# Two unread half-precision products ahead of the scores of four attention steps

## The chip, the cores and the metric

The kernel runs on one core of one Trainium2 chip. The metric is the device time of one execution in microseconds (us); the time of a kernel is the median of several executions. Five engines work side by side, each through its own queue in order: TensorE (PE in the profile, its weight loads PEld), VectorE (DVE), ScalarE (ACT), GpSimd (POOL) and SyncE (SP), whose queue issues the DMA transfers. They meet at semaphores.

## What is computed

Attention over 4 batches, 8 heads, 576 positions of 64 elements, with a position bias that a small network makes out of the distance of two positions; and behind it a feed-forward block of 512 to 2048 to 512 with a squared relu, over all 2304 rows:

```python
scores = scale * np.matmul(q, k.transpose(0, 1, 3, 2))
x = (psi_rel / psi_i)[..., None]          # logs of distance and position
bias = np.maximum(x @ w1 + b1, 0.0) @ w2  # one number for each pair and head
scores = scores + bias.transpose(2, 0, 1)[None, :, :, :]
attn = np.exp(scores - np.max(scores, axis=-1, keepdims=True))
attn = attn / (np.sum(attn, axis=-1, keepdims=True) + 1e-09)
out = np.matmul(attn, v)
...
h = np.maximum(x @ w_in, 0.0)             # x: out, heads side by side
return (h * h @ w_out).astype(np.float32)
```

## The kernel before

The batches are taken in two pairs `p`; the rows of a pair are cut into five blocks `c` (block 0 holds the last 64 rows of both batches, blocks 1 to 4 hold 128 rows of each). A step `t` of the main loop is one (p, c, head); there are 80. The blocks of the first pair go in the order 0, 3, 2, 4, 1, so steps 0 to 7 are block 0, and steps 8 to 15 are block 3 with heads 0 to 7.

A step has these parts. `qk` makes the scores on PE: queries and keys are split into a high and a low half-precision part, and three products of parts are added (high by high, high by low, low by high). In block 0 that is line 413. In the other blocks the 64 columns in the middle of both batches come from line 419 (three products of 128 columns), and the 512 other columns of each batch from line 425 (six products of 512 columns, two at a time on the two halves of the array's rows). All of it goes to one PSUM tile `sc` of 1536 columns, three banks of 512. In a block other than 0 the columns 0 to 575 and 960 to 1535 are used; columns 576 to 959, in the middle bank, are not. There is one `sc`, so the scores of a step wait until DVE has read those of the step before.

`softmax_a` takes the scores with the bias (`s`, line 441, DVE) and the exponent (line 447, ACT). `softmax_b` makes the transpose of the result: in the first two blocks (steps 0 to 15) with float32 transposes on PE (`tp`, lines 459 and 463) that ACT copies out to `at` (lines 460, 464); in the later ones with half-precision parts (`a`, POOL lines 473 and 474) and a transposing DMA. `pv` (line 506), three steps later, multiplies with the values; in steps 0 to 15 in float32.

Beside the steps run the bias (tiles `hg` on DVE and ACT, lines 307 and 309; products `bp` on PE, line 348; copies `be` on ACT, line 369; a DMA to memory and back), the feed-forward block as soon as a block's rows are there (`hp`, line 560, then `g` on ACT, DVE and POOL, then `o`, line 583), and the splitting of the weights, 32 pieces in all: three DVE operations (`ci` lines 223 and 224, `cv` line 226), a cast on ACT (`winH`, `woutH`, line 129) and two POOL operations (scaling `cv` in place, line 131, and the low part, line 242). POOL also splits the values `v` of the first pair, which were read in float32: it casts the high part (`v`, half precision, line 131), scales the float32 tile in place (`v` on `v`, line 131), subtracts (line 154) and clears a corner (line 160). `cv`, the bias copies `be` and two tiles of the feed-forward block take their buffers from one pool of five. The scaling of values in place may only run when the product `pv` that still reads the float32 tile is done: head 0's after step 8's `pv`, head 1's after step 9's, and so on.

The order of the instructions in each queue isn't written by hand. The kernel is built with a scheduler that puts every instruction on an assumed timeline, by the priority `tc.cur_priority` at which it was written and the numbers in `PLACE`, and from that timeline come the queues' orders and the turn in which buffers are taken. An added instruction therefore may move others. `now[0]` is the step that is being written.

Of the kernel before, what the change touches and what calls it, by code (L numbers as in the profile page):

```python
# [51 lines left out]
def tile_attention_moe(  # L52
# [11 lines left out]
    nc = tc.nc  # L64
# [53 lines left out]
    sc = ps_sc.tile([128, 1536], F32, name="sc")  # L118

    now = [0]  # L120
# [281 lines left out]
    def qk(p, c, h):  # L402
        kt = k_t[p, h]
        qt = q_t[p, c, h // 4]
        if h % 4 == 3:
            q_t.pop((p, c, h // 4))
        qs = slice(128 * (h % 4), 128 * (h % 4) + 128)
        terms = ((0, 0), (0, 1), (1, 0))
        if c == 0:
            for n, (qz, z) in enumerate(terms):  # L410
                o = 960 * (h % 2)
                for c0, m in ((0, 64), (64, 512)) if h % 2 else ((0, 512), (512, 64)):
                    nc.tensor.matmul(out=sc[:, o + c0:o + c0 + m], lhsT=qt[:, qz, qs], rhs=kt[:, z, c0:c0 + m],  # L413
                                     start=(n == 0), stop=(n == 2))
        else:

            mid = sc[:, 512:1408].rearrange("p (b j) -> p b j", b=2)[:, :, 0:64]
            for n, (qz, z) in enumerate(terms):
                nc.tensor.matmul(out=mid, lhsT=qt[:, qz, qs], rhs=kz[:, (p * 8 + h) % NKZ, z, :],  # L419
                                 start=(n == 0), stop=(n == 2))  # L420

            for n, (qz, z) in enumerate(terms):
                for b in range(2):
                    r = slice(64 * b, 64 * b + 64)
                    nc.tensor.matmul(out=sc[:, 1024 * b:1024 * b + 512], lhsT=qt[r, qz, qs],  # L425
                                     rhs=kt[r, z, 64 * b:64 * b + 512],
                                     start=(n == 0), stop=(n == 2), tile_position=(64 * b, 0))
# [349 lines left out]
    for t in range(NS + LAG):  # L777
# [5 lines left out]
        if t < NS:  # L783
            p, c, h = steps[t]
            with place("qk"):
                qk(p, c, h)
            with place("sa"):
                softmax_a(p, c, h)
            if t + 2 < NS:
                bias_ld(*steps[t + 2])  # L790
            if h % 4 == 2 and t + 2 < NS:
                q_split(*qlist[(t + 2) // 4])
                q_next()
            if len(moe) > BACKLOG:
                moe_unit()
            softmax_b(p, c, h)
            if last < 0 or steps[last][2] != H - 1:
                moe_unit()
# [77 lines left out]
```

## Time and profile before

| | us |
|---|---|
| median of 3 executions | 655.32 (654.44 to 657.93) |
| the profiled execution | 661.45 |
| its span, first to last instruction | 659.70 |
| PE busy in the span | 615.1 (93%) |
| DVE, ACT, POOL busy | 407.1, 388.1, 376.5 |
| mean granted TensorE clock | 0.965 |

The span is read in two parts. Up to about 110 us DVE is busy nearly without a gap and PE has idle time; from there on PE has hardly any. [...] A row of the timeline gives the start, the time until the end of the last of its instructions, the engine, the line and how many instructions were merged; a bracket is idle time of the engine ahead of it, and what ended it.

### The profile page before, as it was taken

How to read it: one execution, taken by the hardware profiler on the slowest of the kernel's cores; microseconds unless marked ns; L12 is line 12 of the kernel's file. 1: busy time of each engine (PE TensorE's matmuls, PEld its weight loads, DVE VectorE, ACT ScalarE, POOL GpSimd, SP SyncE). 2: the span in 40 equal slices, each digit the busy share in tenths (PEclk: the TensorE clock that was granted, in tenths of full speed). 3: DMA queues.
4: the chain of work that ended last, by engine and by line, in shares of the span. 5: the costliest groups of instructions: out<-in, count | busy, mean ns of one | idle time of the engine just before them, and what ended most of it. 6: DMA issues, size and time to landing. Idle time of an engine off the chain costs nothing.

```text
span 659.7 us, 15574 instructions
## 1 busy us (share of the span) xinstructions
PE 615.1 (93%) x6056; PEld 394.8 (60%) x6056; DVE 407.1 (62%) x813; ACT 388.1 (59%) x856; POOL 376.5 (57%) x394
## 2 busy tenths in 40 slices
PE   5565798999899999999899999999999999999997
PEld 2223356766455566666576676676676676767664
DVE  7997999888864765585856447346545642632321
ACT  5587978788776476656656655656465564342111
POOL 2757578899665456756775465555464663432221
PEclk9698967999999999999899999999999999999999
DMA  7999888477876787889978778679787777524000
GB/s 237 278 294 319 268 255 248 155 209 178 197 173 152 162 193 176 179 180 226 221 170 158 167 134 174 140 169 153 139 172 134 154 149 155 122 56 86 17 34 16
DMA packets 206568, 112.16 MB, mean 170 GB/s; under 512 B 167072, under 2 KB 183456, under 8 KB 206496
## 3 DMA queue, kind: packets, MB, share of 16 engines
q1 hardware_dynamic: 206496, 111.19, 72.0%
q8 instruction: 47, 0.77, 0.5%
q14 instruction: 25, 0.20, 0.1%
HBM read 55.44 MB, written 15.61 MB: 108 GB/s over the span
## 4 chain that ended last, share of the span: by engine, by line
PE 69%; DVE 5%; DMA 4%; issue 2%; ACT 1%; POOL 1%; DVEq 0%; POOLq 0%; ACTq 0%
PE o L583 26%; PE hp L560 26%; PE pv L506 8%; PE sc L425 5%; PE bp L348 2%; DMA at<-a 2%; DVE hg L309 1%; PE sc L419 1%; PE sc L413 1%; DMA xt<-xh 1%; DMA stg<-vd 1%; DVE s L441 1%; DVE cv L226 0%; DVE ci L224 0%; ACT a L129 0%
## 5 line engine op out<-in xcount | busy, mean ns | idle before, releaser
L560 PE MATMUL hp<-xt,winH 128*128 128x256 f16 (+1 forms) x1280 | 195.9, 263 | 0.0
L583 PE MATMUL o<-woutH,g 128*128 128x512 f16 x576 | 185.6, 382 | 4.0 <-ACT o L590 2.2
L560 PE MATMUL hp<-xt,winL 128*128 128x256 f16 (+1 forms) x640 | 162.8, 263 | 0.0
L583 PEld LDWEIGHTS <-g 128*128 128x128 f16 x864 | 82.8, 98 | 97.0 <-issue 11.5
L560 PEld LDWEIGHTS <-winH 128*128 128x128 f16 x1280 | 117.0, 99 | 30.0 <-issue 13.6
L441 DVE CUSTOM_DVE_ANT_0 s<-sc,bt 128x576 f32<-128x576 f32 x144 | 103.5, 751 | 44.1 <-PE sc L425 34.2
L474 POOL TENSOR_TENSOR a<-s,a 128x1024 f16<-128x1024 f32 (+1 forms) x64 | 130.3, 2036 | 0.0
L568 DVE TENSOR_TENSOR r<-hp,r 128x512 f32<-128x512 f32 (+1 forms) x80 | 50.6, 632 | 118.7 <-ACT r L566 118.6
L570 POOL TENSOR_TENSOR g<-r,g 128x512 f16<-128x512 f32 (+1 forms) x80 | 86.7, 1084 | 59.1 <-DVE g L133 48.4
L447 ACT ACTIVATE s<-s,nm 128x576 f32<-128x576 f32 x144 | 111.3, 773 | 6.4
L583 PE MATMUL o<-woutL,g 128*128 128x512 f16 x288 | 109.8, 381 | 0.0
L473 POOL TENSOR_TENSOR a<-s,a 128x128 f16<-128x128 f32 (+1 forms) x64 | 28.1, 440 | 140.4 <-ACT a L129 135.5
L445 ACT ACTIVATE nm<-mx,esc 128x1 f32<-128x1 f32 x144 | 40.9, 288 | 110.8 <-DVE mx L441 110.5
L506 PE MATMUL pv<-v,at 128*128 128x64 f16 (+5 forms) x2112 | 97.9, 207 | 0.5 <-ACT at L460 0.5
L129 ACT ACTIVATE a<-s 128x1152 f16<-128x1152 f32 (+1 forms) x64 | 70.5, 1102 | 44.6 <-DMA at<-a 43.6
L566 ACT ACTIVATE r<-hp 128x512 f32<-128x512 f32 (+1 forms) x80 | 43.1, 539 | 49.6 <-PE hp L560 49.6
L506 PEld LDWEIGHTS <-at 128*128 128x128 f16 (+1 forms) x1792 | 58.3, 100 | 20.2 <-issue 8.6
L560 PEld LDWEIGHTS <-winL 128*128 128x128 f16 x640 | 62.9, 98 | 5.8
L309 DVE TENSOR_SCALAR hg<-tab_t 128x464 f32<-128x464 f32 (+17 forms) x86 | 58.9, 729 | 11.5 <-PE bp L348 11.4
L425 PE MATMUL sc<-k,q 64*128 64x512 f16 x384 | 55.6, 387 | 0.0
L369 ACT ACTIVATE be<-bp,hcst,rows_s 128x288 f32<-128x288 f32 (+29 forms) x67 | 35.8, 571 | 16.5 <-PE bp L348 11.1
L348 PE MATMUL bp<-hg,w2s 128*32 128x288 f32 (+15 forms) x152 | 36.1, 546 | 6.1 <-ACT hg L303 2.4
(88 smaller groups left out, 688.7 us busy)
## 6 DMA issues: line engine op xcount, KB each, us to landing
bt<-biasd SPq DMA_DIRECT2D x64, 288.0 KB, 3.3
stg<-w_in SPq DMA_DIRECT2D x16, 512.0 KB, 5.1
stg<-w_out SPq DMA_DIRECT2D x16, 512.0 KB, 4.7
bt<-biasd SPq DMA_DIRECT2D x32, 144.0 KB, 3.4
qst<-qd SPq DMA_DIRECT2D x32, 128.0 KB, 3.5
out<-o SPq DMA_DIRECT2D x16, 256.0 KB, 2.4
v<-vd SPq DMA_DIRECT2D x8, 320.0 KB, 4.9
stg<-vd SPq DMA_DIRECT2D x8, 320.0 KB, 4.3
```

Source lines behind the costliest of these rows:

```text
L129: nc.scalar.activation(out=out, in_=in_, func=AF.Copy, scale=scale)
L309: nc.vector.tensor_scalar(ht, src, scl[:, n:n + 1], None, op0=ALU.min)
L348: nc.tensor.matmul(out=bp[32 * t:32 * t + 32, 0:d1 - d0], lhsT=w2s if gi < 4 or PATS[z][t] == "A" else w2n, rhs=ts_[t][:, d0:d1], start=Tr ...
L425: nc.tensor.matmul(out=sc[:, 1024 * b:1024 * b + 512], lhsT=qt[r, qz, qs], rhs=kt[r, z, 64 * b:64 * b + 512], start=(n == 0), stop=(n == 2 ...
L441: nc.vector.tensor_tensor_reduce(s[:, 576 * b:576 * b + 576], sc[:, 960 * sb:960 * sb + 576], bt, inv, -3.0e38, ALU.add, ALU.max, mx[:, b: ...
L447: nc.scalar.activation(out=sl, in_=sl, func=AF.Exp, bias=nm[:, b:b + 1], accum_out=su[:, h, b:b + 1])
L474: nc.gpsimd.tensor_tensor(av[:, :, 640:1152], ev[:, :, 0:512], av[:, :, 0:512], op=ALU.subtract)
L506: nc.tensor.matmul(out=dst, lhsT=lhsT, rhs=vt[r, 5 * b + blk, :] if f32 else vt[:, vz, 5 * b + blk, :], start=(n == 0), stop=(n == nt - 1) ...
L560: nc.tensor.matmul(out=hp[:, f * T:f * T + T].rearrange("p (b t) -> p b t", b=nb), lhsT=wt[:, k, c0:c0 + 128], rhs=xt[:, 0:nb, z * 4 + k, ...
L568: nc.vector.tensor_tensor(rr, hp[:, 0:2 * T], rr, op=ALU.mult)
L570: nc.gpsimd.tensor_tensor(g[:, 1, 0:2 * T], r[:, 0:2 * T], g[:, 0, 0:2 * T], op=ALU.subtract)
L583: nc.tensor.matmul(out=blk["o"][b], lhsT=g[:, z, c0:c0 + 128], rhs=wt[:, 2 * u + f, :], start=(u == 0 and f == 0 and z == 0 and wt is wout ...
```

## The change

At the head of `qk`, before a step's scores, two products are added in steps 9 to 12 (block 3, heads 1 to 4): the high part of the queries (128 by 128) with the first 384 columns of the high part of the step's keys, half precision, over all 128 rows of the array, to columns 576 to 959 of `sc`. Nothing reads them.

```diff
         terms = ((0, 0), (0, 1), (1, 0))
+        if 9 <= now[0] < 13:
+            for _ in range(2):
+                nc.tensor.matmul(out=sc[:, 576:960], lhsT=qt[:, 0, qs], rhs=kt[:, 0, 0:384], start=True, stop=True)
         if c == 0:
```

So 8 products and 8 weight loads are added, and no instruction is removed. With them the scheduler gives other orders: PE's differ from step 9 to about step 23, DVE's, ACT's, POOL's and SP's from about step 11 to step 22; the later part of each queue is the same. In the changed program lines from 411 on have a number higher by 3.

On PE, around the scores of step 10 (with what each instruction waits for). Before:

```order
236 L463 MATMUL tp<-ident,s 64x128 [waits Activation_49]
237 L419 LDWEIGHTS q
238 L419 MATMUL sc<-kz,q 128x2x64 [waits DVE_49]
239 L419 LDWEIGHTS q
240 L419 MATMUL sc<-kz,q 128x2x64
```

And now:

```order
240 L466 MATMUL tp<-ident,s 64x128 [waits Activation_49]
241 L411 LDWEIGHTS q
242 L411 MATMUL sc<-k,q 128x384 [waits DVE_49]
243 L411 LDWEIGHTS q
244 L411 MATMUL sc<-k,q 128x384
245 L422 LDWEIGHTS q
246 L422 MATMUL sc<-kz,q 128x2x64
```

The two products (line 411) stand straight ahead of the scores (line 419, now 422), and the wait for DVE that the first score product had is now at the first of them. It is so in steps 9 to 12, in step 11 with one transpose between the two.

On DVE, between the softmax of step 12 (the first pair of line 441, now 444) and that of step 13 (the second pair). The numbers behind the names tell the pieces apart. Before:

```order
158 L441 ISA s_1421,mx_1422<-sc_141,bt_1208 128x576
...
162 L226 SCALAR_TENSOR_TENSOR cv_1180<-stg_1094,ci_1181 128x512
163 L309 TENSOR_SCALAR hg_1273<-tab_t_129 128x352 x2
164 L223 TENSOR_SCALAR ci_1277<-stg_1104 128x512
165 L224 SCALAR_TENSOR_TENSOR ci_1277<-stg_1104,ci_1277 128x512
166 L226 SCALAR_TENSOR_TENSOR cv_1276<-stg_1104,ci_1277 128x512
167 L223 TENSOR_SCALAR ci_1287<-stg_1178 128x512
168 L441 ISA s_1536,mx_1537<-sc_141,bt_1314 128x576
```

And now:

```order
153 L444 ISA s_1429,mx_1430<-sc_141,bt_1212 128x576
...
158 L226 SCALAR_TENSOR_TENSOR cv_1172<-stg_1019,ci_1173 128x512
159 L309 TENSOR_SCALAR hg_1277<-tab_t_129 128x352 x2
160 L223 TENSOR_SCALAR ci_1183<-stg_1094 128x512
161 L224 SCALAR_TENSOR_TENSOR ci_1183<-stg_1094,ci_1183 128x512
162 L226 SCALAR_TENSOR_TENSOR cv_1182<-stg_1094,ci_1183 128x512
163 L444 ISA s_1544,mx_1545<-sc_141,bt_1320 128x576
```

The softmax of step 13 now stands behind the piece from `stg_1094`; before, the next piece (`stg_1104`) and the first operation of the one after it stood ahead of it too: four operations of the splitting have moved behind it.

On POOL, behind the low part of the piece `cv_1086`. `v_332` and `v_414` are the float32 values of heads 1 and 2, which `pv` of steps 9 and 10 reads. Before:

```order
78 L242 TENSOR_TENSOR woutL_127<-cv_1086,woutH_126 128x512
79 L131 TENSOR_SCALAR cv_1096<-cv_1096 128x512
80 L242 TENSOR_TENSOR winL_125<-cv_1096,winH_124 128x2x256
81 L131 TENSOR_SCALAR cv_1170<-cv_1170 128x512
82 L131 TENSOR_SCALAR v_332<-v_332 128x640
83 L242 TENSOR_TENSOR winL_125<-cv_1170,winH_124 128x2x256
84 L154 TENSOR_TENSOR v_2054<-v_332,v_2054 128x640
85 L131 TENSOR_SCALAR cv_1180<-cv_1180 128x512
...
89 L131 TENSOR_SCALAR v_414<-v_414 128x640
```

And now:

```order
78 L242 TENSOR_TENSOR woutL_127<-cv_1086,woutH_126 128x512
79 L131 TENSOR_SCALAR v_332<-v_332 128x640
80 L154 TENSOR_TENSOR v_2062<-v_332,v_2062 128x640
81 L131 TENSOR_SCALAR cv_1096<-cv_1096 128x512
82 L160 MEMSET v_2062 64x2x64
83 L131 TENSOR_SCALAR v_2148<-v_414 128x640
84 L242 TENSOR_TENSOR winL_125<-cv_1096,winH_124 128x2x256
85 L131 TENSOR_SCALAR v_414<-v_414 128x640
```

The scaling of `v_414`, which waits for the product of step 10, comes after six instructions instead of ten; the weights' parts that stood ahead of it (from `cv_1170` and `cv_1180` on) come behind it.

## Rows read from the trace of the kernel before

**Rows 1.** The page: granted clock of TensorE in 40 slices, in tenths.

```profile
PEclk9698967999999999999899999999999999999999
```

**Rows 2.** Stretches of 10 us: PE, PEld, DVE, ACT, POOL busy (x instructions); PEclk, DMA, GB/s.

```profile
80.00:90.00 10.00, 7.59 (x41) 4.66 (x40) 9.97 (x23) 8.99 (x24) 4.97 (x5) 0.76 0.89 259
...
100.00:110.00 10.00, 7.87 (x47) 5.88 (x45) 9.83 (x18) 8.27 (x22) 8.29 (x9) 0.78 0.82 251
110.00:120.00 10.00, 10.00 (x76) 7.33 (x77) 7.78 (x15) 7.97 (x20) 8.53 (x13) 0.71 0.60 184
...
130.00:140.00 10.00, 9.02 (x79) 6.03 (x79) 9.83 (x18) 7.41 (x19) 9.53 (x12) 1.00 0.87 250
...
160.00:170.00 10.00, 8.82 (x113) 4.81 (x110) 10.00 (x17) 6.82 (x16) 9.85 (x10) 1.00 1.03 221
```

**Rows 3.** The same for the single microseconds in which the granted clock changes.

```profile
85.00:86.00 1.00, 1.00 (x7) 1.00 (x7) 1.00 (x3) 0.98 (x3) 0.92 (x1) 0.55 0.96 362
95.00:96.00 1.00, 1.00 (x6) 0.54 (x6) 0.93 (x3) 0.90 (x2) 1.00 (x2) 0.83 0.90 329
105.00:106.00 1.00, 1.00 (x13) 0.72 (x5) 0.96 (x3) 1.00 (x4) 0.94 (x1) 0.79 1.03 340
115.00:116.00 1.00, 1.00 (x14) 1.00 (x11) 0.90 (x4) 0.98 (x3) 1.00 (x1) 0.59 0.49 193
```

**Rows 4.** Timeline of PE: scores of steps 10 to 13, values' products, a wait.

```profile
80.58 0.82 PE L425 MATMUL sc<-k,q 64*128 64x512 f16 x6
...
93.44 1.46 PE L425 MATMUL sc<-k,q 64*128 64x512 f16 x5
...
101.47 0.61 PE L425 MATMUL sc<-k,q 64*128 64x512 f16 x4
...
103.53 0.66 PE L459 MATMUL tp<-ident,s 128*128 128x128 f32 x4 [1.29 <-ACT be L369]
...
108.46 2.42 PE L506 MATMUL pv<-v,at 128*128 128x64 f32 x10
111.25 1.46 PE L425 MATMUL sc<-k,q 64*128 64x512 f16 x6
...
118.06 1.47 PE L506 MATMUL pv<-v,at 128*128 128x64 f32 x10
```

**Rows 5.** Waits of PE from 72 to 105 us: total, times, longest.

```profile
PE tp L459 <- ACT be L369: 2.2, 2, 1.3
```

**Rows 6.** Timeline of DVE.

```profile
112.39 0.69 DVE L223 TENSOR_SCALAR ci<-stg 128x512 uint32<-128x512 uint32 x1
113.80 0.76 DVE L441 CUSTOM_DVE_ANT_0 s<-sc,bt 128x576 f32<-128x576 f32 x1 [0.71 <-PE tp L459]
...
118.25 1.51 DVE L309 TENSOR_SCALAR hg<-tab_t 128x336 f32<-128x336 f32 x2 [1.23 <-PE bp L348]
...
148.90 0.76 DVE L441 CUSTOM_DVE_ANT_0 s<-sc,bt 128x576 f32<-128x576 f32 x1 [1.99 <-PE tp L463]
...
151.50 0.42 DVE L568 TENSOR_TENSOR r<-hp,r 128x256 f32<-128x256 f32 x1 [1.15 <-ACT r L566]
```

**Rows 7.** Timeline of POOL.

```profile
101.41 1.38 POOL L242 TENSOR_TENSOR woutL<-cv,woutH 128x512 f16<-128x512 f32 x1
104.08 0.62 POOL L131 TENSOR_SCALAR cv<-cv 128x512 f32<-128x512 f32 x1 [1.29 <-ACT winH L129]
...
106.72 0.72 POOL L131 TENSOR_SCALAR v<-v 128x640 f32<-128x640 f32 x1
107.41 1.16 POOL L242 TENSOR_TENSOR winL<-cv,winH 128x512 f16<-128x512 f32 x1
108.53 1.50 POOL L154 TENSOR_TENSOR v<-v 128x640 f16<-128x640 f32 x1
110.62 0.62 POOL L131 TENSOR_SCALAR cv<-cv 128x512 f32<-128x512 f32 x1 [0.59 <-ACT woutH L129]
```

**Rows 8.** Waits of PE from 105 to 180 us: total, times, longest.

```profile
PE o L583 <- POOL g L570: 1.8, 2, 1.2
```

## Prediction

> **What bounds the kernel now.** I read the page's line of the granted clock first, then the busy times in stretches of 10 us, then the timelines of PE, DVE and POOL in the stretch that the change touches.
>
> From about 110 us on PE has hardly any gap: the span's later part is a row of products of which the change touches only the first piece. So the question is how much earlier or later PE gets to that piece, whose order is the same before and after. Up to there it is not PE that is full. From 80 to 90 and from 100 to 110 us DVE is busy 9.97 and 9.83 of 10 us, PE 7.59 and 7.87 [rows 2]: DVE sets the pace and PE waits here and there. Between 110 and 120 the roles change: PE 10.00, DVE 7.78.
>
> PE's 10.00 is not all work, though, since the clock is low there. The page shows the early slices under full speed [rows 1], and the single microseconds give the moments [rows 3]. In the microsecond from 85 the mean is 0.55, so nine tenths of it were at the lower level and the fall was at about 85.1; in that from 95 it is 0.83, so the return was at about 95.3. In the same way the second low stretch is from about 105.6 to 115.8. Both last 10.2 us. Where do they lie against the scores? Step 10's began their last part at 80.58 and took 0.82, so they ended at 81.4, 3.7 us ahead of the first fall; step 11's, five of the six products from 93.44 to 94.9, are the work behind which the clock came back; step 12's end at 102.1, 3.5 us ahead of the second fall; step 13's end at 112.7, 3.1 us ahead of the second return [rows 4]. What lies between step 10's scores and step 11's, and between step 12's and step 13's, is float32 work: transposes, the bias and the values' products.
>
> **The change part by part.** Removed: nothing. Added: eight products of 384 columns, each with a weight load.
>
> Their own price. Six products of 512 columns take 0.82 us at full clock, two at a time, so one turn of 512 is at most 0.27; 384 columns are 0.21. At the low clock the six took 1.46, one turn is 0.49, and 384 columns are 0.37 [rows 4]. Steps 9, 10 and 12 are at full clock, 6 x 0.21 = 1.2; step 11's scores are at the low one, 2 x 0.37 = 0.7. Together 1.9 us of PE, an upper bound, as a part of each turn is the way out of the array. How much of it is on the path? The order shows that the products stand behind the same wait for DVE as the scores, so they don't fill the idle time ahead of the scores but lengthen what comes behind it. But behind each there is a wait of PE that a later PE uses up: two waits for ACT's copies of the bias give 2.2 us before 105 [rows 5], the second, 1.29 us at 103.53, right behind step 12's scores [rows 4]. ACT's copies there come behind their own queue, not behind these scores. On the other side of the scores stands DVE's softmax; step 10's and 11's are taken by DVE some us after the scores are there, as DVE is full. So I take 0 for the products; it is 1.9 if ACT's copies turn out to hang on the delayed scores.
>
> [...] The order shows that the unused columns don't free the products from the wait for DVE. [...]
>
> What is moved on DVE. Four operations of the weights' splitting have gone behind the softmax of step 13, 0.69 us each [rows 6], 2.8 us in all. In the trace DVE came to that softmax at 113.09 and waited 0.71 us for PE [rows 6], since PE did step 13's scores at the low clock. DVE will now come there at 110.3 and wait 3.5 us: 2.8 us more idle. Behind it, it gets 0.3 back: the two softmaxes of 0.76 from 113.80 end at 115.3, three operations now stand ahead of `hg`, 2.1 us, so DVE reaches it at 117.4 and waits about 0.9 for the bias product instead of 1.23 [rows 6]. So DVE is some 2.5 us behind at 118 us, and it has next to no gap in which to make that up: 9.83 of 10 us from 130 to 140 [rows 2]. What takes it up: two waits of DVE for others at 148.90 and 151.50, 1.99 and 1.15 us, 3.1 together [rows 6]. What passes to PE before that is between 0 (PE has other work in its queue, the steps' results are wanted three steps later) and 2.5. I take 0.5, nearer to the first, because of that lag of three steps.
>
> What is moved on POOL. The low part of `cv_1086` ended at 102.79 (101.41 + 1.38) [rows 7]. Behind it now come: scaling of head 1's values 0.72, the subtraction 1.50, a scaling of `cv` 0.62, a small clearing, a cast of values like the scaling, 0.72, and a low part 1.16 [rows 7]: 4.7 us. So POOL comes to head 2's scaling at 107.5, and must wait for step 10's product, which ended at 108.46 + 2.42 = 110.88 [rows 4]: 3.4 us. Before, it waited in this place twice for ACT's casts, 1.29 and 0.59 us [rows 7], which now have time. Net 3.4 - 1.9 = 1.5 us later. POOL's next tasks are the same kinds; it is full then (9.53 of 10 us from 130 to 140, 9.85 from 160 to 170 [rows 2]), and PE waits twice for it between 105 and 180 us, 1.8 us in all [rows 8]. The scheduler has changed POOL's order there too, so this wait may go to nothing (-1.8) or take all of the lag (+1.5). I take +0.5, between the ends: POOL has no gap for its lag to vanish in [rows 2], but its order at those two waits is a new one.
>
> Sum: 0 + 0.5 + 0.5 = **+1.0 us**. The profiled execution, 661.45 us by itself, would give 662.4; it stands 6.1 us above the median of the runs shown, 655.32, and since the stretches that I use are early and the added time is no share of the span, the same +1.0 goes on the median: **656.3 us**, 0.15% slower. The bounds: lowest -1.8, highest 1.9 + 2.5 + 1.5 = 5.9. A measurement of this kernel can't tell 0.5%, or 3.3 us, from no change.
>
> **The rivals.**
>
> Faster, by the clock. The added products are work for PE next to the scores, and behind scores the clock came back. If they keep it at 1.00 through the second low stretch, PE gains there: ten values' products took 2.42 us at the low clock and 1.47 at the high one [rows 4], so 10.2 us of such work becomes 6.2, a gain of 4.0. The new waits of DVE and POOL would go too, as they wait for those products. Against it: the falls came 3.5 to 3.7 us after scores, in float32 work, and the new products are not put there but straight ahead of scores, 0.4 us at full clock. In the first low stretch nothing is to be had, since DVE is full. In the second DVE has only 0.71 + 1.23 = 1.94 us of idle time to give [rows 6]. So -1.9 to -4.0 us: 653.4 to 651.3. [...]
>
> Slower, by POOL. POOL's queue is in order; while it waits for head 2's values, the weights' parts behind it wait, and their `cv` buffers, five in all and shared with the bias and the feed-forward block, stay taken. DVE's `cv` then waits for a buffer, and with it the softmaxes that stand behind it. This decides the time as soon as POOL's lag is more than what DVE can run ahead, about the 3.1 us of its later waits. The next head's values give the same wait again: 1.5 us for head 2 and as much for head 3, with 2.5 of DVE's, is 5.5: 660.8.
>
> The change does nothing for the clock and nothing is moved that counts: the products' own 0 to 1.9 us, 655.3 to 657.2. It lies within the forecast's band.
>
> **How the numbers follow.** The forecast, with the third case in it, has 0.54; all of it is within 0.5%. The clock, or an order that happens to fit better, has 0.22, of which 0.16 is beyond 3.3 us (it needs nearly all of the 4.0, or the 1.8 of POOL's wait with it) and 0.06 within. POOL's wait has 0.24, of which 0.21 is beyond and 0.03 within. So faster 0.16, within 0.5% 0.63, slower 0.21. The range: downward to the clock's 4.0 with a part of POOL's 1.8, 650.0; upward to the sum's upper bound, 655.3 + 5.9 = 661.2, taken as 661.0. What is left out is a tenth on each side.
>
> **What would show it.** In the changed kernel the added products should take 0.2 us each at full clock, directly behind a wait for DVE, and the wait for ACT behind step 12's scores should be shorter. The granted clock should still show two low stretches of about 10 us between 80 and 120 us; if the second is gone or short, the clock's rival is right. DVE should wait over 3 us at step 13's softmax; POOL should wait some 3 us for head 2's values behind the product of step 10. If POOL's waits are there and DVE's `cv` shows waits for POOL, the time goes to the slower rival; if PE's two waits for `g` are gone, it goes below the forecast. It would be wrong altogether if PE's later part, behind step 23, took another time: its order is the same.

## The result, and the profile after

The changed kernel took 660.42 us (median of 8 runs, 659.49 to 664.78), the kernel before 656.87 (8 runs, 654.44 to 659.85): a ratio of **1.0064, 95% interval 1.0035 to 1.0093**, some 3 to 4 us slower (the means differ by 4.2 ± 0.9). A second set gave 1.0054 (1.0034 to 1.0074), +3.0 ± 0.4. The prediction was +1.0 us, with a change within 0.5% as the likeliest. The time lies in its range, but the loss is three to four times the one forecast.

The two profiled executions alone would mislead: after's took 659.49 us, before's 661.45. I compare them by the start of each step's scores. At step 8, ahead of any change, after was already 3.4 us ahead (69.12 against 72.49); at step 23 it was 1.2 us behind (193.98 against 192.78). From there on PE has the same products without a gap, except at one place near 316 us. So the change cost this pair 4.6 us between steps 8 and 23; the second profiles of the two kernels (`e1_again`, `e3_before`) give 4.2, 124.25 against 120.04. PE's idle time in that piece is the same, 9.4 us before and 9.2 after (summed from PE's rows).

It holds a wait that doesn't count as idle, though. Each set of four bias products reads four tiles `hg`. Before, the four products of 480 columns ran side by side:

```profile
167.00 0.59 PE L348 MATMUL bp<-hg,w2s 128*32 128x480 f32 x1
167.01 0.60 PE L348 MATMUL bp<-hg,w2n 128*32 128x480 f32 x3
```

After, PE comes to them while DVE still makes the tiles, and they run one behind another:

```profile
165.99 3.32 DVE L309 TENSOR_SCALAR hg<-tab_t 128x480 f32<-128x480 f32 x3
167.64 0.59 PE L348 MATMUL bp<-hg,w2s 128*32 128x480 f32 x1
168.47 1.88 PE L348 MATMUL bp<-hg,w2n 128*32 128x480 f32 x5
```

With the next set, of 496 columns, that is 5.2 us from first start to last end against 2.1 before, and it is so in all four profiles of the new order. The three waits of PE that before has in this place (1.18 and 0.61 us for POOL, 0.95 for ACT) are gone in return, and one of 1.1 us for DVE has come.

The page of after: busy times and granted clock.

```profile
span 657.8 us, 15567 instructions
PE 615.8 (94%) x6064; PEld 396.6 (60%) x6064; DVE 403.4 (61%) x813; ACT 387.5 (59%) x856; POOL 378.4 (58%) x394
...
PEclk9698977799999999999999999999999999999999
```

The stretches of after, with the columns of [rows 2].

```profile
80.00:90.00 10.00, 6.82 (x51) 4.37 (x50) 9.83 (x20) 8.10 (x20) 6.78 (x7) 1.00 0.98 270
100.00:110.00 10.00, 10.00 (x51) 6.58 (x48) 6.94 (x15) 6.11 (x15) 4.75 (x7) 0.58 0.64 176
110.00:120.00 10.00, 8.48 (x78) 6.49 (x76) 8.78 (x17) 7.71 (x18) 9.36 (x12) 0.93 0.51 142
130.00:140.00 10.00, 9.89 (x86) 6.61 (x85) 8.70 (x16) 6.56 (x16) 8.92 (x13) 1.00 0.70 218
```

From 100 to 110 us PE is now full at the low clock (0.58), and DVE and POOL, 9.83 and 8.29 before [rows 2], have fallen to 6.94 and 4.75: they wait for PE. The products on PE, of steps 9 and 12, with the scores behind them:

```profile
73.60 0.48 PE L411 MATMUL sc<-k,q 128*128 128x384 f16 x2 [0.96 <-DVE mx L444]
73.92 0.33 PE L422 MATMUL sc<-kz,q 128*128 128x128 f16 x3
...
98.00 0.82 PE L411 MATMUL sc<-k,q 128*128 128x384 f16 x2
98.62 0.53 PE L422 MATMUL sc<-kz,q 128*128 128x128 f16 x3
```

The pair delays the scores by 0.32 us at the full clock, 0.62 at the low one, 1.6 us in all four steps. It stands behind the wait for DVE (0.96), not in it. Timelines of POOL and DVE at the moved work:

```profile
103.25 1.16 POOL L242 TENSOR_TENSOR winL<-cv,winH 128x512 f16<-128x512 f32 x1
109.34 0.72 POOL L131 TENSOR_SCALAR v<-v 128x640 f32<-128x640 f32 x1 [4.93 <-PE pv L509]
```

```profile
106.55 0.72 DVE L309 TENSOR_SCALAR hg<-tab_t 128x352 f32<-128x352 f32 x2 [1.93 <-PE bp L348]
...
110.83 0.76 DVE L444 CUSTOM_DVE_ANT_0 s<-sc,bt 128x576 f32<-128x576 f32 x1 [1.44 <-PE tp L462]
```

POOL waits 4.93 us for step 10's values' product, where it had waited 1.29 and 0.59 for ACT [rows 7].

### The profile page after: what moved, and what is told of

It is laid out like the page before. It is cut to its first block, busy times and chain, and to the rows that moved or that the text cites. A ratio compares the mean times of both kernels' runs of the same rounds, so it can differ in the third digit from the quotient of the medians.

```text
span 657.8 us, 15567 instructions
## 1 busy us (share of the span) xinstructions
PE 615.8 (94%) x6064; PEld 396.6 (60%) x6064; DVE 403.4 (61%) x813; ACT 387.5 (59%) x856; POOL 378.4 (58%) x394
## 4 chain that ended last, share of the span: by engine, by line
PE 65%; DMA 10%; DVE 8%; POOL 6%; ACT 6%; issue 5%; SPq 0%; DVEq 0%; POOLq 0%; ACTq 0%
PE hp L563 23%; PE o L586 22%; PE pv L509 8%; PE sc L428 5%; DMA at<-a 5%; PE bp L348 4%; POOL a L477 2%; DMA biasd<-be 2%; DVE hg L309 2%; PE tp L462 1%; DVE s L444 1%; PE sc L422 1%; ACT a L129 1%; ACT be L369 1%; ACT s L450 1%
## 5 line engine op out<-in xcount | busy, mean ns | idle before, releaser
L309 DVE TENSOR_SCALAR hg<-tab_t 128x464 f32<-128x464 f32 (+17 forms) x86 | 54.1, 676 | 10.0 <-PE bp L348 9.8
L428 PE MATMUL sc<-k,q 64*128 64x512 f16 x384 | 54.2, 383 | 0.0
```

What stands on the lines that cost most here:

```text
L309: nc.vector.tensor_scalar(ht, src, scl[:, n:n + 1], None, op0=ALU.min)
```

## The experiments

Below, "+2.0 ± 0.3 us" is the mean of a kernel's runs less the mean of the runs of before that were taken beside them, with its standard error; where two kernels of one set are compared, their means are. A ratio has its 95% interval.

To part the order from the products, each kernel of this kind holds an order on every engine by dependencies without semaphores, from each instruction to the one ahead of it:

```
+    for row in ROWS:                       # one list of instructions per engine
+        for a, b in zip(row, row[1:]):
+            tc.add_manual_dep(made[b], a, NoSync)
```

**1. Order or products.** `e1_order` has after's order and narrow products; `e1_products` before's order and the wide ones, `e1_twice` twice as many of them.

```
-                nc.tensor.matmul(out=sc[:, 576:960], lhsT=qt[:, 0, qs], rhs=kt[:, 0, 0:384], start=True, stop=True)
+                nc.tensor.matmul(out=sc[:, 576:592], lhsT=qt[:, 0, qs], rhs=kt[:, 0, 0:16], start=True, stop=True)
```

> The changed kernel once more, as the measure for the other three. Every theory: 3 to 5 us above the kernel before (the first comparison gave a ratio of 1.0064).

> The changed kernel's order of instructions on every engine, held by dependencies on the instruction ahead, but the eight products are 16 columns wide instead of 384. Theory 'order': the loss comes from the moved instructions on DVE, POOL, ACT and SP, so 3 to 5 us above the kernel before. Rival 'products': the loss is the time that the products take on TensorE ahead of the scores (1.6 us in the changed kernel's trace from their starts to those of the scores) and what follows from it, so within 1 us of the kernel before. Rival 'both': 1 to 3 us above.

> The order of the kernel before on every engine, held in the same way, with the eight products of 384 columns straight ahead of the scores of steps 9 to 12. Theory 'order': within 1 us of the kernel before. Rival 'products': 2 to 5 us above (1.6 us of the products, the rest by lost clock). Rival 'both': 1 to 2.5 us above.

> As the run before, with four products of 384 columns in each of steps 9 to 12 instead of two, sixteen in all. Theory 'order': within 1 us of the kernel before, as these products stand where TensorE waits. Rival 'products': twice the loss of the run with eight, 4 to 8 us above. Rival 'both': 2.5 to 5 us above.

Measured: the changed kernel again 1.0054 (1.0034 to 1.0074), +3.0 ± 0.4; the order with narrow products 1.0048 (1.0021 to 1.0075), +3.3 ± 0.8; the products in before's order 1.0045 (1.0023 to 1.0068), +2.6 ± 0.7; twice as many 1.0033 (1.0008 to 1.0058), +1.7 ± 0.8. Either part alone brings nearly the whole loss, and twice the products do not bring twice of it: no theory fits all four. What the order and the products have in common is eight products more on PE.

**2. The control, and engines set back one by one,** all with narrow products. `e2_order_before` has before's order everywhere; the others keep after's order on ACT and POOL. Setting only these two back was not tried.

> Control: the order of the kernel before on every engine, held by the same dependencies as in the other runs, with the eight products 16 columns wide. Theory 'order' and theory 'products' both: within 1 us of the kernel before, as neither the order nor any time on TensorE is changed. Rival 'any change': holding the order, or eight instructions more of whatever width, costs 2 to 3 us by itself, so 2 to 3 us above.

> Products 16 columns wide; ACT and POOL in the order of the changed kernel, TensorE, DVE and SP in that of the kernel before. Theory 'POOL waits': the scaling that stands ahead of two other transfers on POOL is what costs, so 2.5 to 4 us above the kernel before. Rival 'TensorE': the order of the products and weight loads on TensorE itself is what costs, so within 1 us.

> Products 16 columns wide; DVE, ACT and POOL in the order of the changed kernel, TensorE and SP in that of the kernel before. Theory 'POOL waits': 2.5 to 4 us above the kernel before. Theory 'DVE': as much, and more than the run with ACT and POOL alone by 1 us or more. Rival 'TensorE': within 1 us.

> Products 16 columns wide; TensorE, ACT, POOL and SP in the order of the changed kernel, DVE in that of the kernel before. Theory 'POOL waits' and rival 'TensorE': 2.5 to 4 us above the kernel before. Theory 'DVE': within 1 us.

Measured: the control 1.0025 (1.0010 to 1.0041), +1.9 ± 0.5. ACT and POOL alone in after's order 1.0186 (1.0144 to 1.0228), +12.6 ± 1.6; with DVE 1.0093 (1.0063 to 1.0122), +6.4 ± 1.0; with PE and SP instead of DVE 1.0145 (1.0118 to 1.0173), +9.9 ± 0.9. So the new orders of ACT and POOL together cost up to 12 us when the other engines don't follow, and each engine that follows takes some back. Which part of it is POOL's new place for the values was not tried by itself. In `e2_actpool` PE waits from 100 to 150 us so (total, times, longest):

```profile
PE hp L614 <- ACT at L514: 3.1, 1, 3.1
PE o L637 <- POOL g L182: 2.6, 1, 2.6
```

The surprise is the control: products that delay the scores by 0.05 us a step, in an unchanged order, cost 1.9 us.

**3. Does it matter where they stand?** Before itself; narrow and wide products in steps 30 to 33, where PE has no gap; the control again.

```
-        if 9 <= now[0] < 13:
+        if 30 <= now[0] < 34:
```

> The kernel before, run as if it were a changed one: shows how far apart two sets of runs of one kernel come, and gives a second profile of it. Every theory: within 0.7 us of the kernel before. Theory 'event' (the profile of before fell on an unlucky stretch at 314 to 322 us): the stretch from the scores of step 38 to those of step 44 takes 43 to 45.5 us here, not 46.4.

> The order of the kernel before on every engine, with the eight products of 16 columns in steps 30 to 33, where TensorE never waits, and none in steps 9 to 12. Theory 'place': the narrow products cost 1.9 us in steps 9 to 12 because of what happens there, so within 0.7 us here (their own time is 8 times 0.025 us). Rival 'any change': sixteen instructions more on TensorE cost 1.5 to 2.5 us wherever they stand.

> The same with 384 columns in steps 30 to 33. Theory 'place': 1.3 us above the kernel before, which is 8 times the 0.16 us that one takes at the full clock, and no more, so 0.7 to 2 us. Rival 'any change': 3 to 4 us above.

> The order of the kernel before with the eight products of 16 columns in steps 9 to 12, once more, to halve the uncertainty of the control. Theory 'place' and rival 'any change': 1 to 2.7 us above the kernel before. Theory 'chance' (the control came out high by its own scatter): within 0.7 us.

Measured: before 1.0009 (0.9992 to 1.0026), +0.8 ± 0.5, and 44.2 us from step 38 to 44, so the 46.4 us of the first profile were an unlucky stretch (in it the granted clock is 0.50 from 317.2 to 320.6 us, behind a wait of 2.2 us for ACT; in no other profile is it low there); narrow late 1.0009 (0.9993 to 1.0026), +0.8 ± 0.5; wide late 1.0032 (1.0017 to 1.0048), +2.3 ± 0.4; narrow in steps 9 to 12 again 1.0027 (1.0007 to 1.0046), +2.1 ± 0.5. Wide less narrow in the late place is 1.5 ± 0.6, the 1.3 us that eight products take. Narrow ones cost nothing there beyond before itself (0.1 ± 0.6), and 1.4 ± 0.6 more than it in steps 9 to 12.

**4. Which steps?** Four narrow products in steps 9 and 10, four in 11 and 12, eight in 14 to 17, and the order alone again.

> The order of the kernel before on every engine, with four products of 16 columns in steps 9 and 10 alone. The eight of steps 9 to 12 cost 1.8 us. Theory 'waiting place': the products cost where TensorE waits for the softmax ahead of the scores, which is steps 9 and 10, so 1.2 to 2.2 us above the kernel before. Rival 'dense place': the cost comes from steps 11 and 12, which lie in the float32 stretch, so within 0.6 us. Rival 'each a little': 0.6 to 1.2 us.

> The same with four products of 16 columns in steps 11 and 12 alone. Theory 'waiting place': within 0.6 us of the kernel before. Rival 'dense place': 1.2 to 2.2 us above. Rival 'each a little': 0.6 to 1.2 us.

> The same with eight products of 16 columns in steps 14 to 17, behind the stretch in which the clock falls. If the cost belongs to steps 9 to 12: within 0.6 us of the kernel before. If it belongs to any step before TensorE is busy without a gap (from some 185 us on): 1.2 to 2.4 us above.

> The changed kernel's order on every engine with products of 16 columns, once more, to halve the uncertainty of its first set. Theory 'order adds' : 1 to 2.5 us more than the same narrow products in the order of before, so 2.8 to 4.3 us above the kernel before. Rival 'the order is free': no more than the narrow products in the order of before, so 1.3 to 2.3 us above.

Measured: 1.0000 (0.9971 to 1.0029), +0.3 ± 0.8; 1.0003 (0.9979 to 1.0028), +0.7 ± 0.7; 1.0011 (0.9987 to 1.0035), +1.1 ± 0.6; the order 1.0030 (1.0003 to 1.0057), +1.8 ± 0.8. Neither half costs clearly what the whole does, so no single place is to blame. With errors of 0.6 to 0.8 the runs alone can't refute "each a little". The traces gave another theory: the scores of step 20 to those of step 21 take 10.6 us in six traces of before's order (before twice, the two late ones, the two halves), and 11.25 to 11.7 in the five with eight or sixteen products ahead of step 20. And in these five a packet of kind `instruction` on queue q8 (16 KB; before's page has 47 of them, 0.77 MB) comes 1.2 to 1.6 us behind the scores of step 20, in the other six 5.6 to 5.9 us behind. Its place moves with the number of PE's instructions ahead of it, so I take it for a fetch of PE's program.

The five also part among themselves. From the scores of step 20 to those of step 22 the six take 17.5 us, two of the five 18.1, and three 19.6 to 19.7. In all five PE's bias product waits 2.0 us for ACT, against 0.9 to 1.0 in the two profiles of before; in the three the granted clock is then at 0.50 for 3.4 us, in the other two it stays at 1.00. So in `e2_order_before`:

```profile
173.61 0.60 PE L399 MATMUL bp<-hg,w2s 128*32 128x496 f32 x1 [2.03 <-ACT be L420]
176.00:177.00 1.00, 1.00 (x8) 0.16 (x5) 0.96 (x2) 1.00 (x2) 0.88 (x2) 0.50 0.87 224
```

**5. The fetch.** From the first such fetch of before (16.28 us) to the last (642.90 us), 46 later, PE starts 11715 products and weight loads, 255 for each fetch, and the two kernels here take it as 256. Eight products are 16 instructions (a weight load and a matmul each). `e5_fill_256` adds 240 idle ones ("fillers") in step 1, meant for the gap of 8 us there, so that the later boundaries are again those of before; `e5_fill_272` adds 256, so that they stay shifted. Both have the eight narrow products and before's order, and differ by 16 instructions in step 1.

```
+        if now[0] == 1:
+            for _ in range(60):            # 64 in e5_fill_272; two passes each
+                nc.tensor.matmul(out=sc[0:32, 576:578], lhsT=w2s, rhs=sm_t[:, 1:3], start=True, stop=True,
+                                 tile_position=(0, 0))
```

> The order of the kernel before on every engine, the eight products of 16 columns in steps 9 to 12, and 60 float32 products of 2 columns that nobody reads in step 1, in the 8 us in which TensorE waits for POOL (some 4 us at 36 ns for each of their two passes). With the eight that makes 256 instructions more on TensorE by step 13, which is the 16 KB that one fetch of its program brings. Theory 'fetch' (the eight products shift the fetch of TensorE's program from 170 to 164 us, into the transposes xh and at, which end later): the fetch falls as in the kernel before, some 2 to 4 us behind the scores of step 20 plus 2, the scores of step 20 to those of step 21 take 10.6 us, and the wait of bp for ACT there is at most 1.0 us; within 0.9 us of the kernel before. Rival 'presence' (the products themselves do it): 11.2 us, a wait of 2.0 us, and 1.3 to 2.5 us above.

> The same with 64 instead of 60 float32 products in step 1, so 272 instructions more by step 13. Theory 'fetch': as with the eight products alone, which are 16 more, so the early fetch, 11.2 us from step 20 to step 21, the wait of 2.0 us, and 0.6 to 1.5 us above the run with 256. Rival 'presence': the same time as the run with 256, within 0.7 us, with the same wait.

Measured: 1.0031 (1.0013 to 1.0048), +2.1 ± 0.4, and 1.0076 (1.0050 to 1.0103), +4.8 ± 0.7 us. So the **16 instructions at the start cost 2.7 ± 0.7 us**, more than the 0.6 to 1.5 expected. The fetch's places (5.8 us behind the scores of step 20 in `e5_fill_256`, as 5.7 in before, and 2.0 in `e5_fill_272`), the times from step 20 to 21 and the waits of `bp` came as the fetch theory had them. The time of `e5_fill_256` did not: it was to be within 0.9 us of before and is no better than the eight narrow products without fillers (+1.9, +2.1). The fillers have a price, since they did not fall into the gap, and each took 0.055 us instead of the 0.036 of the eight of their form at 2.81 us of `e1_again` (0.29 us). They wait for DVE like the scores and stand behind it; first `e5_fill_256`, then `e5_fill_272`:

```profile
23.17 6.56 PE L641 MATMUL sc<-sm_t,w2s 128*32 128x2 f32 x120 [7.77 <-DVE mx L678]
23.25 6.99 PE L641 MATMUL sc<-sm_t,w2s 128*32 128x2 f32 x128 [7.77 <-DVE mx L678]
```

The scores behind them start at 29.66 and 30.17 us, in before at 23.88. How much of that lasts no run shows; step 8 starts at 74.40 and 73.14 us in these two profiles, at 69.1 to 73.7 in the others. So no run shows that putting the fetch back gives the time back. The 16 instructions in question took 0.43 us themselves, and that is made up by 35.7 us, where the two profiles stand level (35.72 and 35.68).

What the DMA queues did from 164 to 169 us: GB/s in 40 equal slices, packets, MB and share of q8 if it had any, and the transposes with their time to landing. First `e5_fill_256`, whose fetch is at 171.28 us, outside the window, then `e5_fill_272`:

```profile
GB/s 134 295 272 329 343 429 274 300 194 9 74 129 55 111 166 295 184 129 313 332 221 209 193 193 199 203 137 102 80 141 197 250 172 226 170 174 244 244 227 104
...
xt<-xh SPq DMA_TRANSPOSE x1, 3.7
at<-a SPq DMA_TRANSPOSE x1, 6.5
```

```profile
GB/s 37 129 129 129 184 221 221 258 350 240 191 180 193 211 207 180 205 37 45 51 47 29 31 18 6 8 10 8 10 10 100 285 291 289 269 283 289 289 293 293
...
q8 instruction: 1, 0.02, 1.2%
...
xt<-xh SPq DMA_TRANSPOSE x1, 4.8
at<-a SPq DMA_TRANSPOSE x1, 5.4
```

In `e5_fill_272` the fetch (at 166.09 us) falls where both transposes are under way (issued at 164.10 and 165.44), and for 1.6 us only 6 to 51 GB/s are moved; the fetch itself took 0.96 us of that (1.2% of 16 engines in 5 us). In `e5_fill_256` it is mostly 100 to 300. `xt` takes 4.8 us to land instead of 3.7, though `at` takes 5.4 instead of 6.5. What follows from the later `xt`, on DVE and then PE, in `e5_fill_256`:

```profile
169.28 0.60 DVE L780 TENSOR_SCALAR xh<-x,cc 128x512 f16<-128x512 f32 x1
```

```profile
168.30 0.39 PE L820 MATMUL o<-woutH,g 128*128 128x512 f16 x1 [1.18 <-POOL g L807]
173.00 0.60 PE L820 MATMUL o<-woutH,g 128*128 128x512 f16 x2 [0.61 <-POOL g L807]
175.04 0.60 PE L578 MATMUL bp<-hg,w2s 128*32 128x496 f32 x1 [0.95 <-ACT be L599]
```

and in `e5_fill_272`:

```profile
168.98 1.61 DVE L780 TENSOR_SCALAR xh<-x,cc 128x512 f16<-128x512 f32 x1 [1.05 <-DMA xt<-xh]
```

```profile
171.18 0.60 PE L820 MATMUL o<-woutH,g 128*128 128x512 f16 x2 [0.17 <-POOL g L807]
174.30 0.60 PE L578 MATMUL bp<-hg,w2s 128*32 128x496 f32 x1 [2.02 <-ACT be L599]
```

The next `xh` waits 1.05 us for `xt` to be read, the softmax behind it on DVE comes later, then ACT's copy, and PE's bias product waits 2.02 instead of 0.95; of that it had gained 0.44 at `o`. Net 0.6 us, which is 11.25 instead of 10.62 from step 20 to 21. The rest of the 2.7 came later in this pair. PE's waits from 300 to 350 us, `e5_fill_256` first:

```profile
PE o L820 <- ACT o L827: 0.5, 1, 0.5
PE pv L743 <- DMA at<-a: 0.3, 1, 0.3
```

```profile
PE o L820 <- ACT o L827: 2.0, 1, 2.0
PE pv L743 <- DMA at<-a: 1.7, 1, 1.7
```

The second has a fetch beside it again: from 331 to 336 us of `e5_fill_272` the transfers go to 0 to 23 GB/s for 1.7 us from the fetch at 333.12 us on, which lies inside the issue of a transpose of `at` (330.20 to 335.03 us); in `e5_fill_256` the fetch at 333.46 fell between two issues.

```profile
GB/s 18 37 37 92 258 258 424 361 277 309 258 274 209 111 63 18 150 0 0 0 0 0 0 0 6 8 8 10 8 10 23 266 291 291 291 293 281 293 293 291
```

At this place the fetch is not enough by itself: in `e3_narrow_late` it lies inside the issue of the same transpose (329.19, in 326.56 to 329.85), and PE doesn't wait for `at` at all.

The first, at 316 us, has no fetch beside it in either trace. It is longer in most kernels with more instructions ahead of it (1.6 to 2.1 us in seven of eight traces, 0.6 in `e3_narrow_late`) than in the others of before's order (0.5 to 1.5 us in four, but 2.2 in the first profile of before). In after's order, with as many more instructions, it is 0.2 to 0.4 in three traces and 1.5 in one; why stays open.

## Why the prediction was wrong

**The products' own price** was bounded by 1.9 us and taken as 0. Wide less narrow is 1.5 ± 0.6 in the late place, 0.6 ± 0.8 in before's order, 0.5 ± 0.7 in after's (the order's two sets together, +2.5 ± 0.5): with their weights 0.9 ± 0.4 for the time on PE. So for that time the bound held and the choice was too low: PE's later waits did not take all of it. A part of a product's time is indeed not in the way of the next: in after the pair of step 9 took 0.48 us and held the scores back by 0.32, that of step 12 0.82 and 0.62. The whole price in before's order, +2.6 ± 0.7, is more; that comes last. The reason that I gave for 0, the wait for ACT behind step 12's scores [rows 5], did get shorter (0.3 us in after from 72 to 105 us), but the time went to other waits; PE's idle time stayed as it was.

**DVE.** A wait of over 3 us at step 13's softmax was forecast; it is 1.44, after 1.93 at `hg`, 3.4 together. Right in kind, and nearly in sum, though more than half came one place earlier. The bias products in a row, shown above, are not a sign of its lag: PE comes to them earlier, 1.3 us behind step 20's scores instead of 3.2. What the lag passed on to PE by itself was not measured.

**POOL.** Forecast a wait of some 3 us for step 10's product; it is 4.93. PE's waits for `g` between 105 and 180 us, 1.8 us [rows 8], are gone, but others of the same size have come:

```profile
PE hp L563 <- ACT at L463: 1.3, 1, 1.3
PE hp L563 <- DVE r L571: 1.1, 1, 1.1
PE tp L462 <- ACT be L369: 0.8, 1, 0.8
```

For the two together I took 0.5 + 0.5. The order's share, products left as they are, is 0.5 ± 0.6 (narrow) and 0.4 ± 0.8 (wide), so 0.5 ± 0.5: the estimate of 1.0 is not refuted. The rival that POOL's queue costs 5.5 us has its wait in the trace, and its time of 660.8 is close to the 660.42 measured, but that is luck: the whole new order, POOL's queue in it, costs 0.5 ± 0.5. `e2_actpool` shows what waits like it can cost, 12.6 us with ACT's order in it, where DVE and PE keep theirs; in the changed kernel they don't.

**The clock.** The rival of a clock kept up fell: in after it is low from about 91.3 to 108.4 us and again from 118.6 to 125.4, 23.9 us between steps 8 and 23, against 20.5 in the first profile of before [rows 3] and 23.9 in the second. So that is scatter: the same program of after's order has 41.0 us of it in the profile of `e1_order` and 10.2 in that of `e4_order`, and takes 127.9 and 120.8 us for these steps. Over all runs of one set the mean granted clock is 0.966 for after, 0.964 for before: no loss there either. Pairs of products of 0.48 to 0.82 us did not keep it up. The moments of the falls and returns in the forecast are worked out from two levels of the clock, 1.00 and 0.50; the stretches of before between them, with the columns of [rows 2], have these:

```profile
86.00:95.00 9.00, 9.00 (x41) 5.76 (x40) 8.69 (x16) 7.17 (x16) 6.68 (x8) 0.50 0.94 258
96.00:105.00 9.00, 6.62 (x58) 4.20 (x55) 8.51 (x17) 7.06 (x16) 7.15 (x10) 1.00 0.85 258
106.00:115.00 9.00, 9.00 (x48) 7.16 (x48) 8.12 (x14) 6.41 (x16) 8.00 (x11) 0.50 0.79 229
```

**The unused columns.** That they don't free the products from the wait for DVE was right: the first of step 9 starts behind a wait of 0.96 us for DVE.

**The step that failed** is the 0 for the products. I costed an added instruction by its time on PE alone, at most 1.9 us, and let PE's later waits take that up. In before's order, where nothing else is changed, the eight products cost 2.6 ± 0.7 us, and still 1.9 ± 0.5 and 2.1 ± 0.5 when they are 16 columns wide and take next to no time (0.05 us a step). So in place of 0 stand 0.9 ± 0.4 for their time on PE, and 1.1 ± 0.4 for their mere presence (eight narrow products ahead of step 20, three sets, less the four sets of before, of the late narrow ones and of the two halves).

For the presence the runs point at the fetch. Each of the eight is also two more instructions of PE's program, and with them the fetch at step 20 lies elsewhere against the DMA transposes, 1.2 to 1.6 us behind the scores instead of 5.6 to 5.9. In before's order the traces show the loss that goes with it at steps 20 and 21, 0.6 us in two profiles and 2.1 to 2.2 in the three where the clock fell too, and the 16 instructions changed by themselves cost 2.7 ± 0.7. Moving only the fetches behind step 33, as the late narrow ones do, cost nothing (0.1 ± 0.6), so a moved fetch is not enough; that it matters which transposes it meets is my reading of the traces, and no run shows it by itself.

For the changed kernel itself that cause is not shown, and its trace speaks against it at step 20. The fetch stands in the same place, 1.1 us behind step 20's scores (167.44 against 166.31), but the transposes beside it land early:

```profile
xt<-xh SPq DMA_TRANSPOSE x1, 3.1
at<-a SPq DMA_TRANSPOSE x1, 4.7
```

From step 20 to 23 it takes 27.7 us against 28.9 before. Its loss in the profile lies ahead of step 20, from step 8 on 97.2 against 91.4 (the part of the work on either side of step 20 differs too, so only the 4.6 in all are a loss), and no run moved a fetch in after's order. Added up afterwards, 0.9 for the products, 0.5 for the order, 0.7 by which kernels without any effect came out above before (before itself among them, +0.8 ± 0.5), and 1.1 carried over from before's order make 3.2 of the 3.0 ± 0.4 and 4.2 ± 0.9 measured. Where the last 1.1 comes from in after's order stays open.

None of the kernels was faster than before.

## What to carry to other kernels

Cost an added instruction twice: by its time on the engine (here 0.9 ± 0.4 us for eight products), and by what its presence does to the work behind it (here 1.1 ± 0.4 in before's order). Where a kernel is slower by a fraction of a per cent after a harmless edit, repeat the edit with instructions that do next to nothing, in the old order; then change only their number. And compare step by step from a common anchor: two single profiles differed here by 3.4 us ahead of the change, as much as its whole effect. An engine that is busy all the time may still be waiting: look whether things that ran side by side now run in a row.

## What the runs showed of the hardware

PE's program of this kernel, as I read the traces, comes in blocks of 16 KB on queue q8, a new one about every 256 instructions: before has 47 of them, 255 products and weight loads apart on average, the kernels with fillers 48, and the 256 instructions more of `e5_fill_256` leave the fetch 5.8 us behind the scores of step 20, where it is 5.7 in before. From 110 to 206 us of before the blocks are 11 to 16 us apart. In the late place moving the fetches cost 0.1 ± 0.6 us. In `e5_fill_272` the 16 instructions that moved them took 2.7 ± 0.7 us. PE waited there for POOL and ACT (1.3 and 2.0 us from 160 to 180 us), and what was late ahead of that is a DMA transpose beside a fetch: `xt` took 4.8 us to land instead of 3.7, and for some 1.6 us transfers fell to 6 to 51 GB/s. The traces show the two together; that the fetch holds the transfers back no run shows by itself.

How far that holds, the 20 traces show together. The transposes `xt` with a fetch in their first 2 us took 4.48 us to land on average (51 of them), the others 3.61 (309). For `at` it is 5.22 (207) against 5.08 (1073). These averages mix places of the kernel. So far as they go, a fetch goes with a later landing at `xt`, and hardly at `at`. Whether other transfers land later beside a fetch was not tried.
